# Sinks copied on chip, keys and queries as pairs of tokens, and a moved start in a fused attention and MLP kernel

## The chip, the cores and the metric

The kernel runs on one core of one Trainium2 chip. The metric is the device time of one execution in microseconds (us). The engines that matter: TensorE (PE in the rows) multiplies matrices, and transposes by multiplying with an identity; VectorE (DVE), ScalarE (ACT) and GpSimd (POOL) work elementwise; SyncE (SP) issues transfers (DMA). TensorE writes into PSUM banks, which the other engines empty.

## The reference, cut to what matters

```python
# q, k, v: 4 x 8 heads x 768 tokens x 64; n_sink = 4, window = 128
scores = q @ k.T / sqrt(64)
keep = (key < n_sink) | (0 <= query - key < window)
a = exp(where(keep, scores, -1e9) - rowmax)
a = a / (sum(a) + 1e-9)
x = (a @ v), heads side by side            # 3072 x 512
h = x @ w_in                               # 512 x 2048, float64 weights
g = h * erf(softplus(h))
out = g @ w_out                            # 2048 x 512, float64 weights
```

## The kernel before, in words

**Tiles and steps.** The 3072 tokens are 12 groups of 256. Attention works on a group's eight heads two at a time, so a group is 4 steps, 48 in all; group 0 is steps 0 to 3, group 1 steps 4 to 7. The numbers behind names (`tp_4`, `ps_4`) are steps. For the MLP a group's hidden layer is 16 chunks of 128 units, two to a PSUM bank: `h_0` holds chunks 0 and 1, `h_2` the next two, up to `h_14`; the gate of `h_0` is `gf_1`, of `h_2` `gf_3`, and so on.

**One step of attention.**
- `prep` transposes the keys and queries of 256 tokens on TensorE (`tqk`, L292) and copies them to `kq` on ScalarE (L295).
- `score` multiplies them (`ps`, L343), masks a triangle on VectorE (COPY_PREDICATED, L356), reduces each row's minimum (L361, results `neg`), and takes exponentials on ScalarE (L365, into `pst`, with row sums in `sum`). From step 3 on the scores of all steps share one PSUM bank pair, so `ps` of a step waits for the reductions of the step before.
- `norm` adds 1e-9 to the sums (L372) and inverts them (L373) on VectorE, multiplies `pst` by them (L378 on ScalarE for steps 2 to 7, VectorE otherwise), and multiplies the sinks' columns (`snk`, L384, VectorE).
- `ptrans` transposes `pst` (`tp`, L396) and `snk` (`ts`, L397) on TensorE. ScalarE copies them to `pa` (L403) and `pz` (L407, L409), and GpSimd selects triangles in both (L414). `tp` and `ts` share two PSUM banks of their kind with `tqk`.
- `av` multiplies by the values (`v_early`, and `vz`, which holds sinks and window halves; L451); `xfin` copies the result to `xf` on ScalarE (L464).

**The MLP.** `hidden` (L639 for group 0, which works in plain fp32; L643 for the others) makes `h` in two PSUM banks; `act` makes the gate with five ScalarE squares and the like (L656 to L661) and three products per bank on VectorE (L665), of which the first reads `h`, so that its end frees the bank for the `h` after next. `project` (L685 for groups 0 and 1) adds into the output banks.

**Weights.** They lie in 8-byte words. 32 blocks of 512 KB are loaded on SP's queue (`ws`), and VectorE makes fp32 of each 128x512 block by three instructions: one TENSOR_SCALAR (L541, "first conversion" below) and two SCALAR_TENSOR_TENSOR (L546, L549). Each block has two halves, so a block is listed as `wf_N` from `ws_N`. This conversion runs through the first 100 us, between the attention's instructions on VectorE.

**The start.** For groups 0 and 1, `early_load` brings keys, queries and values with 256-byte pieces; `early_sinks` brings the 4 sinks' rows (16 lanes each) into `vz` by eight small DMAs, and `early_dup` copies halves of `vz` on GpSimd.

**What sets the order.** `plan` gives each stage of each step a due slot, `at` turns the slot and the stage's offset (`O`, and `E` for slots below `EA`) into a priority, and a list of stages sorts inside one slot. A scheduler then orders each engine's instructions at build time by these priorities and its own estimate of times; `follow` pins one instruction behind another on its engine. Engines run their queues in order.

## Time and profile before

| | us |
|---|---|
| median of 3 runs | 741.97 (741.89 to 742.29) |
| the profiled execution | 741.58 |
| its span | 739.5 |
| TensorE busy | 716.2 (97% of the span) |
| ScalarE busy | 552.0 (75%) |
| VectorE busy | 486.6 (66%) |
| GpSimd busy | 204.8 (28%) |
| granted TensorE clock, mean | 0.994 |

The busy shares are means over a start of some 100 us, in which VectorE is full and TensorE waits now and then, and a long rest, in which TensorE is always busy. The rows below are of the start. In a timeline row the number in brackets at the end is the time for which that engine idled before the row, and the name behind the arrow is what released it. A row with "x16" holds sixteen instructions in a row, and its duration runs from the first one's start to the last one's end; one multiplication in fp32 shows as two instructions, a transpose as one. As instructions overlap in the pipeline, the time of one is best read from start to start.

### The profile page before, as it was taken

To read this page: it belongs to the slowest core of one execution; us is meant where nothing else is said; L and a number is where in the kernel's file an instruction comes from. 1 tells how busy PE (TensorE), PEld (TensorE's weight loads), DVE (VectorE), ACT (ScalarE), POOL (GpSimd) and SP (SyncE) were. 2 spreads that over 40 slices of the span, in tenths; PEclk is the share of its full clock that TensorE was granted. 3 is DMA by queue.
4 is the path that set the end of the run, shared out by engine and by line. 5 is a ranking of instruction groups with operands and counts; after the bars stand their busy time and mean duration, and the time that the engine had idled before them with its cause. 6 is when DMAs were issued, how large, how long until landed. Compare 5 with 4: busy or idle time off the path is not lost. (4 is left out here: it accounts for less than half of the span.)

```text
span 739.5 us, 16417 instructions
## 1 busy us (share of the span) xinstructions
PE 716.2 (97%) x5808; PEld 596.2 (81%) x5808; DVE 486.6 (66%) x1367; ACT 552.0 (75%) x1313; POOL 204.8 (28%) x302
## 2 busy tenths in 40 slices
PE   6779899999999999999999999999999999999997
PEld 3556567766888888888888888888888888899885
DVE  8899987765786675665666665665666566475252
ACT  5676759974986966976885975976886886776573
POOL 3311132111332432332233242234224223333221
PEclk9899999999999999999999999999999999999999
DMA  7998011122212222212212311211221221200000
GB/s 182 319 373 305 16 35 47 32 54 47 73 40 58 66 47 54 64 37 55 75 34 55 82 38 44 76 41 39 77 52 37 79 55 38 63 17 2 29 1 34
DMA packets 113001, 53.07 MB, mean 72 GB/s; under 512 B 91728, under 2 KB 105552, under 8 KB 112912
## 3 DMA queue, kind: packets, MB, share of 16 engines
q1 hardware_dynamic: 112352, 51.87, 26.0%
q8 instruction: 49, 0.80, 0.5%
q14 instruction: 40, 0.33, 0.2%
q10 hardware_dynamic: 560, 0.07, 0.1%
HBM read 38.01 MB, written 6.29 MB: 60 GB/s over the span
## 5 line engine op out<-in xcount | busy, mean ns | idle before, releaser
L643 PE MATMUL h<-xh,wt 128*128 128x256 f32 x1408 | 277.8, 285 | 0.2 <-DVE u L665 0.2
L643 PEld LDWEIGHTS h<-xh,wt 128*128 128x128 f32 x1408 | 223.9, 188 | 7.0 <-issue 1.1
L673 POOL TENSOR_TENSOR g<-u,g 128x512 fp32r<-128x512 f32 x80 | 106.0, 1325 | 340.6 <-DVE g L672 336.9
L643 PE MATMUL h<-xl,wt 128*128 128x256 f32 x704 | 197.8, 282 | 0.0
L661 ACT ACTIVATE u<-r 128x512 f32<-128x512 f32 x288 | 161.6, 622 | 10.3 <-DVE gf L665 3.1
L643 PEld LDWEIGHTS h<-xl,wt 128*128 128x128 f32 x704 | 132.1, 188 | 4.8 <-issue 1.0
L665 DVE SCALAR_TENSOR_TENSOR u<-u,u 128x512 f32<-128x512 f32 x160 | 125.6, 785 | 14.9 <-ACT u L661 0.9
L689 PE MATMUL o<-wt,g 128*128 128x512 f32 x320 | 127.4, 398 | 0.0
L688 PE MATMUL o<-wt,g 128*128 128x512 f32 x320 | 127.3, 398 | 0.0
L690 PE MATMUL o<-wt,g 128*128 128x512 f32 x320 | 123.6, 397 | 0.2 <-POOLq L811 0.2
L665 DVE SCALAR_TENSOR_TENSOR u<-u,h 128x512 f32<-128x512 f32 x80 | 54.9, 686 | 83.1 <-ACT u L661 80.6
L414 POOL TENSOR_SCALAR_AFFINE_SELECT pz<-pa 64x256 f32<-64x256 f32 (+1 forms) x96 | 50.9, 530 | 157.1 <-ACT pa L403 153.8
L365 ACT ACTIVATE pst<-pst,neg 128x144 f32<-128x144 f32 x192 | 77.5, 407 | 19.3 <-DVE neg L361 18.3
L656 ACT ACTIVATE r<-h 128x512 f32<-128x512 f32 x96 | 56.7, 590 | 20.3 <-PE h L643 15.7
L688 PEld LDWEIGHTS o<-wt,g 128*128 128x128 f32 x320 | 60.0, 187 | 11.5 <-ACT ot L694 0.4
L690 PEld LDWEIGHTS o<-wt,g 128*128 128x128 f32 x320 | 59.0, 187 | 12.5 <-POOLq L811 0.7
L689 PEld LDWEIGHTS o<-wt,g 128*128 128x128 f32 x320 | 60.0, 188 | 10.6
L672 DVE CAST g<-u 128x512 fp32r<-128x512 f32 x80 | 34.8, 434 | 47.5 <-PE o L690 44.7
L657 ACT ACTIVATE r<-r 128x512 f32<-128x512 f32 x96 | 60.7, 632 | 2.6
L658 ACT ACTIVATE r<-r 128x512 f32<-128x512 f32 x96 | 60.7, 632 | 2.5
L685 PE MATMUL o<-wf,gf 128*128 128x512 f32 x128 | 58.8, 595 | 1.7 <-DVE gf L665 1.7
L295 ACT COPY kq<-tqk 128x512 f32<-128x512 f32 x48 | 27.9, 582 | 36.3 <-PE tqk L292 34.1
(88 smaller groups left out, 938.0 us busy)
## 6 DMA issues: line engine op xcount, KB each, us to landing
ws<-in_moe_w_in_dram SPq DMA_DIRECT2D x16, 512.0 KB, 7.2
ws<-in_moe_w_out_dram SPq DMA_DIRECT2D x16, 512.0 KB, 8.2
out_dram<-ot SPq DMA_DIRECT2D x24, 256.0 KB, 2.3
v<-in_v_dram SPq DMA_DIRECT2D x56, 96.0 KB, 2.2
q<-in_q_dram SPq DMA_DIRECT2D x80, 64.0 KB, 2.1
k<-in_k_dram SPq DMA_DIRECT2D x80, 64.0 KB, 2.1
vz<-v SPq DMA_DIRECT2D x80, 64.0 KB, 2.1
kq<-kq SPq DMA_DIRECT2D x28, 64.0 KB, 2.0
```

Of the source, the lines that this page charges most:

```text
L365: nc.scalar.activation(y, y, AF.Exp, bias=d["neg"][:, i, h : h + 1], scale=-1.0, accum_out=d["sum"][:, i, h : h + 1])
L643: last = nc.tensor.matmul(o, wt[NC * j + c][:, p, fs], xt[e][:, c, :], start=(m == 0), stop=(m == len(ops) - 1))
L656: nc.scalar.activation(r, h, AF.Tanh, bias=b_t, scale=0.5)
L657: nc.scalar.activation(r, r, AF.Square, bias=b_v, scale=-0.5)
L658: nc.scalar.activation(r, r, AF.Square, bias=b_r)
L661: sq = nc.scalar.activation(u, r, AF.Square, bias=b_a[i], scale=CS)
L665: pr = nc.vector.scalar_tensor_tensor(out=acc, in0=u, scalar=CC[i] * CS**2, in1=x, op0=ALU.add, op1=ALU.mult)
L673: nc.gpsimd.tensor_tensor(gl, acc, gh.bitcast(F32), op=ALU.subtract)
L685: nc.tensor.matmul(o, gt[0][:, ws], wf[16 + f], start=(f == 0), stop=(f == NF - 1))
L688: behind(nc.tensor.matmul(o, gh[:, ws], wt[16 + f][:, 0, :], start=(f == 0), stop=False))
L689: nc.tensor.matmul(o, gh[:, ws], wt[16 + f][:, 1, :], start=False, stop=False)
L690: nc.tensor.matmul(o, gl[:, ws], wt[16 + f][:, 0, :], start=False, stop=(f == NF - 1))
```

## The change

1. **Sinks.** Four of the eight sink DMAs are gone; GpSimd copies the rows from the other half of `vz` (`early_dup`, z = 2). The zero fill of that half is dropped.
2. **Pairs of tokens.** Group 1's keys and queries are loaded with two neighbouring tokens on a partition, in two DMAs of 512-byte pieces instead of four of 256-byte pieces. `prep` turns them with eight ordinary matmuls per step, 64 output partitions each, in alternate halves, instead of four transposes, and ScalarE puts them in order with two strided copies instead of one.
3. **Step 1 first on ScalarE.** Step 2's `norm` moves behind `ptrans` in its slot (`norm2`); `follow` puts step 2's multiplies behind step 1's `pz` copies, step 3's exponentials behind step 2's multiplies, and step 2's transposes behind step 0's values.
4. **Slots.** `ptrans` of steps 4 to 7 is due one slot later, `prep` of steps 4 and 5 is due in slot 5 instead of 4, and `EA` goes from 12 to 6.
5. **The addition of 1e-9** for steps 4 to 7 goes from VectorE to ScalarE.

```diff
-PW, EA = 256, 12
+PW, EA = 256, 6
...
-            nc.vector.memset(vz[: P // 2, 1], 0.0)
...
+                if nm != "v" and g:
+                    t = t.rearrange("p (h j d) -> p h j d", h=H, j=2)
...
+                if nm != "v" and g:
+                    x = src[0, hs, g * GT : (g + 1) * GT].rearrange("h (p j) d -> p h (j d)", j=2)
+                    nc.sync.dma_start(t[:, hs].rearrange("p h j d -> p h (j d)"), x)
+                    return
...
-                if z:
+                if z == 2:
+                    nc.gpsimd.tensor_copy(vz[lo, 1], vz[hi, 0])
+                elif z:
...
+                if g == 1:
+                    prev = None
+                    for n, t in enumerate((d["k"], d["q"])):
+                        for j in range(2):
+                            for h in range(2):
+                                prev = follow(prev, nc.tensor.matmul(
+                                    tp[64 * h : 64 * h + 64, 2 * n + j, :], t[:, h, j], ident, start=True, stop=True
+                                ))
+                    for n in range(2):
+                        y = kq[:, c, 1 + 2 * n : 3 + 2 * n, :P].rearrange("p b (t j) -> p b j t", j=2)
+                        nc.scalar.copy(y, tp[:, 2 * n : 2 * n + 2, :].rearrange("p j (b t) -> p b j t", b=2))
+                    return
...
-                        nc.scalar.activation(
+                        follow(mark["n"] if s == 3 else None, nc.scalar.activation(
...
-                follow(mark["t", 2] if s == 1 else None, nc.vector.tensor_scalar_add(sm, sm, 1.0e-9))
+                if NE <= s < NA:
+                    nc.scalar.activation(sm, sm, AF.Identity, bias=1.0e-9)
+                else:
+                    follow(mark["t", 2] if s == 1 else None, nc.vector.tensor_scalar_add(sm, sm, 1.0e-9))
...
-                            nc.scalar.mul(p, p, sm[:, i, h : h + 1])
+                            mark["n"] = follow(mark["z"] if s == 2 else None, nc.scalar.mul(p, p, sm[:, i, h : h + 1]))
...
-                        mark["p", s] = nc.tensor.transpose(out=tp[:, h, i, :], in_=pst[:, s % RING, i, h, :P], identity=ident)
+                        x = nc.tensor.transpose(out=tp[:, h, i, :], in_=pst[:, s % RING, i, h, :P], identity=ident)
+                        mark["p", s] = follow(mark["v"] if s == 2 else None, x)
...
-                    nc.scalar.copy(pz[hf, :, :, other], y.broadcast_to([HP, 2, 2, HP]))
+                    mark["z"] = nc.scalar.copy(pz[hf, :, :, other], y.broadcast_to([HP, 2, 2, HP]))
...
-                prev = mark.get(("p", s + 1)) if 0 < s < NE - 1 else None
+                prev = mark.get(("p", s + 1)) if s == 2 else None
...
+                mark["v"] = prev
...
-                        ("prep", prep, max(4, s - 1) if NE <= s < 2 * NPAIR else pos(s) - 3), ("norm", norm, pos(s) + 1 + (s == 1)), ("ptrans", ptrans, pos(s) + 2),
+                        ("prep", prep, max(5, s - 1) if NE <= s < 2 * NPAIR else pos(s) - 3), ("norm" if s != 2 else "norm2", norm, pos(s) + 1 + (s == 1)), ("ptrans", ptrans, pos(s) + 2 + (NE <= s < 2 * NPAIR)),
...
-            STAGES = ("xfin", "norm", "ptrans", "av", "kcopy", "prep", "core", "dup", "load")
+            STAGES = ("xfin", "norm", "ptrans", "norm2", "av", "kcopy", "prep", "core", "dup", "load")
...
-            head += [(early_sinks, z, i, h) for z in range(2) for i in range(2) for h in range(2)]
+            head += [(early_sinks, 0, i, h) for i in range(2) for h in range(2)]
...
-            for z in range(2):
+            for z in range(3):
                 plan.setdefault(0, []).append(("kcopy", lambda s: early_dup(s), z))
```

The order shows what the moves come to. First ScalarE's queue behind the exponentials of step 2, before:

```order
L365 ACTIVATE pst_132,sum_2_304<-pst_132,neg_2_305 128x144 x4
L464 COPY xf_0_408<-av_0_362 128x256
L378 ACTIVATE pst_132<-pst_132,sum_2_304 128x128 x4
L403 COPY pa_1_351<-tp_1_344 128x512
L409 COPY pz_1_352<-tp_1_344 64x2x64
L365 ACTIVATE pst_132,sum_3_376<-pst_132,neg_3_377 128x144
L407 COPY pz_1_352<-ts_1_345 64x4x64 x2
L365 ACTIVATE pst_132,sum_3_376<-pst_132,neg_3_377 128x144 x3
L403 COPY pa_2_425<-tp_2_418 128x512
```

and after the change (line numbers of the changed kernel are higher; L403, L378, L365 and L464 are L430, L404, L388 and L492 there):

```order
L388 ACTIVATE pst_131,sum_2_298<-pst_131,neg_2_299 128x144 x4
L430 COPY pa_1_337<-tp_1_330 128x512
L436 COPY pz_1_338<-tp_1_330 64x2x64
L434 COPY pz_1_338<-ts_1_331 64x4x64 x2
L404 ACTIVATE pst_131<-pst_131,sum_2_298 128x128 x4
L388 ACTIVATE pst_131,sum_3_370<-pst_131,neg_3_371 128x144 x4
L404 ACTIVATE pst_131<-pst_131,sum_3_370 128x128 x4
L492 COPY xf_0_402<-av_0_356 128x256
L430 COPY pa_2_419<-tp_2_412 128x512
```

Step 1's three copies stand ahead of step 2's four multiplies, the four exponentials of step 3 behind these, and the copy of step 0's output (`xf_0`) behind step 3's multiplies.

Next VectorE's queue around the masked copies of step 4's scores (`ps_4`) and the first of the four reductions, before:

```order
L541 TENSOR_SCALAR wf_16_579<-ws_16_183 128x512
L546 SCALAR_TENSOR_TENSOR wf_6_558<-ws_7_178,wf_6_558 128x512
L546 SCALAR_TENSOR_TENSOR wf_16_579<-ws_16_183,wf_16_579 128x512
L356 COPY_PREDICATED ps_4_539<-tri_125,ps_4_539 64x2x2x64
L549 SCALAR_TENSOR_TENSOR wf_6_558<-ws_7_178,wf_6_558 128x512
L541 TENSOR_SCALAR wf_16_579<-ws_17_272 128x512
L549 SCALAR_TENSOR_TENSOR wf_16_579<-ws_16_183,wf_16_579 128x512
L356 COPY_PREDICATED ps_4_539<-tri_125,ps_4_539 64x2x2x64
L541 TENSOR_SCALAR wf_18_609<-ws_18_274 128x512
L546 SCALAR_TENSOR_TENSOR wf_16_579<-ws_17_272,wf_16_579 128x512
L361 ISA pst_132,neg_4_538<-ps_4_539,mask_78 128x144
```

and after:

```order
L569 TENSOR_SCALAR wf_8_655<-ws_8_400 128x512
L574 SCALAR_TENSOR_TENSOR wf_18_607<-ws_19_394,wf_18_607 128x512
L574 SCALAR_TENSOR_TENSOR wf_8_655<-ws_8_400,wf_8_655 128x512
L577 SCALAR_TENSOR_TENSOR wf_18_607<-ws_19_394,wf_18_607 128x512
L379 COPY_PREDICATED ps_4_553<-tri_125,ps_4_553 64x2x2x64
L569 TENSOR_SCALAR wf_8_655<-ws_9_447 128x512
L577 SCALAR_TENSOR_TENSOR wf_8_655<-ws_8_400,wf_8_655 128x512
L569 TENSOR_SCALAR wf_10_680<-ws_10_453 128x512
L379 COPY_PREDICATED ps_4_553<-tri_125,ps_4_553 64x2x2x64
L574 SCALAR_TENSOR_TENSOR wf_8_655<-ws_9_447,wf_8_655 128x512
L574 SCALAR_TENSOR_TENSOR wf_10_680<-ws_10_453,wf_10_680 128x512
L384 ISA pst_131,neg_4_552<-ps_4_553,mask_78 128x144
```

The blocks `wf_18` (from `ws_18` and `ws_19`), `wf_8` and part of `wf_10` now stand ahead of the first reduction: between step 3's sinks and that reduction there are 12 first conversions and 22 second or third ones, where there were 8 and 13.

Last TensorE's queue around step 4's transposes (`tp_4`), where `ps_5` is the scores of step 5, before:

```order
L343 MATMUL ps_5_622<-kq_128 64x224 x2
L396 MATMUL tp_4_590<-ident_61,pst_132 128x128 x2
L639 MATMUL h_4_816<-xf_0_408,wf_4_467 128x256 x2
L639 MATMUL h_4_816<-xf_0_408,wf_6_558 128x256 x2
L639 MATMUL h_4_816<-xf_0_408,wf_4_467 128x256 x2
L639 MATMUL h_4_816<-xf_0_408,wf_6_558 128x256 x2
L396 MATMUL tp_4_590<-ident_61,pst_132 128x128 x2
L397 MATMUL ts_4_591<-ident_61,snk_4_576 128x128
L685 MATMUL o_0_0_852<-wf_16_579,gf_1_713 128x512
```

and after:

```order
L366 MATMUL ps_5_636<-kq_128 64x224 x2
L422 MATMUL tp_4_618<-ident_61,pst_131 128x128 x3
L667 MATMUL h_4_830<-xf_0_402,wf_4_449 128x256 x2
L667 MATMUL h_4_830<-xf_0_402,wf_6_572 128x256 x2
L667 MATMUL h_4_830<-xf_0_402,wf_4_449 128x256 x2
L667 MATMUL h_4_830<-xf_0_402,wf_6_572 128x256 x2
L422 MATMUL tp_4_618<-ident_61,pst_131 128x128
L424 MATMUL ts_4_619<-ident_61,snk_4_590 128x128
L366 MATMUL ps_6_762<-kq_128 64x208 x2
L366 MATMUL ps_6_762<-kq_128 64x224 x2
```

Three of the four transposes of step 4 now stand ahead of `h_4`, and the scores of step 6 ahead of the first output products (`o`).

## Rows read from the trace of the kernel before

**Rows 1.** Table of stretches: us, busy time of each engine (instructions), granted clock, DMA share, GB/s.

```profile
24.00:25.00 1.00, 0.21 (x2) 0.21 (x4) 1.00 (x2) 1.00 (x6) 0.87 (x3) 0.67 1.04 208
25.00:31.00 6.00, 6.00 (x38) 4.74 (x37) 5.64 (x13) 4.18 (x12) 2.51 (x6) 0.50 0.97 312
31.00:32.00 1.00, 1.00 (x7) 0.79 (x6) 1.00 (x3) 0.00 (x0) 0.00 (x0) 0.92 1.31 259
100.00:120.00 20.00, 20.00 (x152) 13.96 (x151) 14.97 (x46) 14.11 (x38) 5.41 (x8) 1.00 0.14 31
```

**Rows 2.** Timeline of TensorE: start, duration, engine, line, operation, tiles, [idle before].

```profile
22.73 0.66 PE L396 MATMUL tp<-ident,pst 128*128 128x128 f32 x4 [2.55 <-ACT pz L409]
24.79 0.70 PE L451 MATMUL av<-pa,v_early 128*64 128x128 f32 x4 [1.40 <-POOL pa L414]
...
34.59 0.44 PE L292 MATMUL tqk<-ident,k_early 128*128 128x128 f32 x2
34.86 0.38 PE L292 MATMUL tqk<-ident,q_early 128*128 128x128 f32 x2
...
36.29 0.64 PE L451 MATMUL av<-pz,vz 128*64 128x64 f32 x16
36.86 5.45 PE L639 MATMUL h<-xf,wf 128*128 128x256 f32 x24
...
45.83 0.62 PE L396 MATMUL tp<-ident,pst 128*128 128x128 f32 x2 [2.61 <-ACT pst L378]
46.33 3.72 PE L639 MATMUL h<-xf,wf 128*128 128x256 f32 x16
...
52.07 3.70 PE L685 MATMUL o<-wf,gf 128*128 128x512 f32 x8 [1.69 <-DVE gf L665]
...
75.87 0.33 PE L396 MATMUL tp<-ident,pst 128*128 128x128 f32 x1 [1.61 <-ACT pst L378]
```

**Rows 3.** The same of TensorE, from 78 us on.

```profile
91.97 3.29 PE L639 MATMUL h<-xf,wf 128*128 128x256 f32 x14 [0.49 <-DVE gf L665]
```

**Rows 4.** Timeline of VectorE from 25 to 46 us.

```profile
25.77 0.38 DVE L384 TENSOR_TENSOR snk<-pst,sum 128x128 f32<-128x128 f32 x1
...
30.09 0.43 DVE L541 TENSOR_SCALAR wf<-ws 128x512 int32<-128x512 int32 x1 [0.23 <-DMA ws<-in_moe_w_in_dram]
...
34.75 0.43 DVE L541 TENSOR_SCALAR wf<-ws 128x512 int32<-128x512 int32 x1 [1.49 <-DMA ws<-in_moe_w_out_dram]
...
39.93 0.31 DVE L361 CUSTOM_DVE_ANT_0 pst<-ps,mask 128x144 f32<-128x144 f32 x1
...
42.05 0.42 DVE L541 TENSOR_SCALAR wf<-ws 128x512 int32<-128x512 int32 x1
42.39 0.68 DVE L549 SCALAR_TENSOR_TENSOR wf<-ws,wf 128x512 int32<-128x512 int32 x1
42.99 0.42 DVE L541 TENSOR_SCALAR wf<-ws 128x512 int32<-128x512 int32 x1
...
45.60 0.68 DVE L665 SCALAR_TENSOR_TENSOR gf<-u,h 128x512 f32<-128x512 f32 x1
```

**Rows 5.** Timeline of ScalarE from 19 to 46 us.

```profile
19.42 0.37 ACT L464 COPY xf<-av 128x256 f32<-128x256 f32 x1
...
40.28 0.41 ACT L365 ACTIVATE pst<-pst,neg 128x144 f32<-128x144 f32 x1 [2.93 <-DVE neg L361]
...
41.88 0.58 ACT L656 ACTIVATE r<-h 128x512 f32<-128x512 f32 x1
...
45.40 0.97 ACT L378 ACTIVATE pst<-pst,sum 128x128 f32<-128x128 f32 x3
```

**Rows 6.** Timeline of GpSimd from 12 to 26 us.

```profile
16.64 0.68 POOL L414 TENSOR_SCALAR_AFFINE_SELECT pz<-pa 64x128 f32<-64x128 f32 x2 [0.79 <-ACT pa L403]
...
22.59 1.45 POOL L414 TENSOR_SCALAR_AFFINE_SELECT pz<-pa 64x128 f32<-64x128 f32 x2 [3.30 <-ACT pa L403]
```

More of the change, by code (lines that the diff above doesn't have):

```diff
@@ L42 @@
 NM, NA = 2, 8
-PW, EA = 256, 12
-O = dict(prep=-100, norm=-100, core=-300, av=-300, load=-400, dup=-100, kcopy=-50, ptrans=-200, xfin=-100,
+PW, EA = 256, 6
+O = dict(prep=-100, norm=-100, norm2=-100, core=-300, av=-300, load=-400, dup=-100, kcopy=-50, ptrans=-200, xfin=-100,
          hid=0, proj=900, res=500, act=-400, wl=100, wc=0, ws=300)
@@ L223, in early_tile @@
                 t = wpool.tile([P, 2 * DM], F32, tag="wo", name=f"{nm}_early{g}")
-                t = early[g, nm] = t.rearrange("p (n h d) -> p n h d", n=2, h=H)
+                if nm != "v" and g:
+                    t = t.rearrange("p (h j d) -> p h j d", h=H, j=2)
+                else:
+                    t = t.rearrange("p (n h d) -> p n h d", n=2, h=H)
+                early[g, nm] = t
                 for c in range(NPAIR):
@@ L228, in early_tile @@
                         d[nm] = [early[0, nm][:, 1, cs] if g else None] + [t[:, n, cs] for n in range(2)]
+                    elif g:
+                        d[nm] = t[:, cs]
                     else:
@@ L364, in score @@
                         )
-                        nc.scalar.activation(
+                        follow(mark["n"] if s == 3 else None, nc.scalar.activation(
                             y, y, AF.Exp, bias=d["neg"][:, i, h : h + 1], scale=-1.0, accum_out=d["sum"][:, i, h : h + 1]
-                        )
+                        ))
             def norm(s):
@@ L371, in norm @@
                 sm = d["sum"]
-                follow(mark["t", 2] if s == 1 else None, nc.vector.tensor_scalar_add(sm, sm, 1.0e-9))
+                if NE <= s < NA:
+                    nc.scalar.activation(sm, sm, AF.Identity, bias=1.0e-9)
+                else:
+                    follow(mark["t", 2] if s == 1 else None, nc.vector.tensor_scalar_add(sm, sm, 1.0e-9))
                 nc.vector.reciprocal(sm, sm)
```

## The prediction

> **What bounds the kernel now.** I read the table of stretches first. From 100 to 120 us TensorE is busy 20.00 of 20 us [rows 1], and from 92 us to the last output it hardly waits. So the time is TensorE's work plus its waits in the first 92 us plus what the half clock costs there, and the reader should look for these two things only.
>
> TensorE's timeline gives the waits. The bracket at a row is the idle time before it. At 22.73 it is 2.55 us (step 1's copies on ScalarE), at 24.79 1.40 (GpSimd's selects), at 45.83 2.61 (step 4's normalised scores), at 52.07 1.69 (the gate of group 0), at 75.87 1.61 [rows 2], and at 91.97 0.49 [rows 3]. That is 10.35 us. After the first two the granted clock is 0.67, then 0.50 from 25 to 31 us, then 0.92 [rows 1]. 0.50 is the lower of its two levels, 1.2 of 2.4 GHz. What is missing to full speed sums to 0.33 + 6 x 0.50 + 0.08 = 3.4 us.
>
> Then VectorE's timeline. It works through the queue of weight conversions almost without a pause; two waits for the DMA, 0.23 and 1.49 us [rows 4], are all it has between step 3's sinks (25.77) and the gate at 45.60. So a place in VectorE's queue is a time, and counting instructions there gives due times. ScalarE, the third view, waits for VectorE at 40.28, 2.93 us, for step 4's reductions [rows 5].
>
> **The change at the start (to 28 us).** Step 1's copies go ahead of step 2's multiplies and of step 3's exponentials on ScalarE; TensorE takes the transposes of step 1 before step 0's products. In the trace of before the 2.55 us wait was for these copies, so it goes. What is late next: step 0's products wait for GpSimd, which now selects for step 1 behind step 0's pair, a wait I put at 1.4 us (a pair of selects takes 0.68, or 1.45 beside conversions [rows 6]). And the copy of step 0's output, at 19.42 in before (0.37 us [rows 5]), now stands behind the multiplies of step 3 on ScalarE, near 27.0; the first hidden product waits for it, 2.9 us. So 3.95 us of waits become about 4.3: no gain, at least none here. The clock may stay up, which would gain up to 3.4 at this place; whether it matters is decided later, since TensorE runs into VectorE's next result anyway.
>
> **Fewer DMAs.** Four sink copies and two loads go from SP's queue. The weights arrive some 2 us earlier (an estimate), and VectorE's two waits, 1.72 us, vanish. GpSimd gets one more copy, while it is idle. The dropped fill costs VectorE nothing.
>
> **Pairs of tokens.** Step 4 to 7's keys and queries are turned by eight half-width products instead of four transposes. Two transposes start 0.27 us before the next two, so four take 0.54 [rows 2]. The nearest rows for the new form: eight 64-column half-width products (16 records) take 0.57 us (36.29 to 36.86), at 128 columns 1.14 per step; not overlapped at all, half of a full-width 256-column product, 5.45 us / 12 / 2 = 0.23 each, 1.8 per step [rows 2]. So 0.6 to 1.3 us more per step, 2.4 to 5.0 in all; I take 2.4, since the products with alternate halves in the rows do overlap. It lies in 28 to 41 us, in front of TensorE's wait for step 4, which has room for it: in before TensorE idled 2.61 us there, and the change lengthens that wait (next part). If that cover is gone, it costs its 2.4. ScalarE copies twice at about 0.37 (the 128x256 copy) instead of once; it idles there.
>
> The Trainium skill bears on this: "TensorEngine Tiling (Array Packing)", Restrictions and Gotchas, says that column tiling can't be used with the transpose mode for fp32 input. So pairs in halves must run as ordinary fp32 products, as the order shows; the rows above price this, and the rule gives no other time.
>
> **Step 4's place in VectorE's queue: the term that decides.** The transposes of steps 4 to 7 come one slot later, step 4's preparation too, and the scheduler fills VectorE with weights before step 4's reductions. From step 3's sinks to the first reduction stand in before 8 first conversions, 13 second or third ones and 2 masked copies; after the change 12, 22 and 2. A first conversion takes 0.34 us (42.05 to 42.39), another 0.60 (42.39 to 42.99), a masked copy some 0.40 (an estimate between these two), a reduction 0.23 [rows 4]. Before: 11.3 us by this count, 26.08 + 11.3 + 1.72 of DMA waits = 39.1, against 39.93 measured, so the count runs 0.85 short. After: 18.0, so 44.1 by bare count, 45.0 with the 0.85, 45.5 with it in proportion. I take 45.0: five us later than 39.93.
>
> From there two chains lead to the first hidden product of chunk 4, at 46.33 in before [rows 2].
> - Scores: from the first exponential (40.28) to the first multiply (45.40) ScalarE took 5.12 us; one square (0.58) leaves that stretch, the sum's addition comes onto ScalarE (some 0.2; between nothing and the 0.37 of a small copy) [rows 5]: 4.7. So 45.3 + 4.7 = 50.0, then 0.43 to the first transpose [rows 2]; the new order wants three transposes instead of two, whose third multiply ends 0.65 later (0.97 for three): 51.1.
> - Gate: the bank that it writes is free when VectorE's first product of the gate is done, in before 45.60 + 0.6. The count for it after is 15, 27, 3 masked copies, 4 reductions and small ones, 23.4 us: 26.08 + 23.4 + 0.6 = 50.1 bare, 51.1 with the shortfall.
>
> Both say about 51.1 for what stood at 46.33: **+4.8 us**. Bounds: 50.1 by bare counts, +3.7; 51.6 in proportion, +5.2.
>
> **After that.** Of before's waits 1.69 + 1.61 + 0.49 = 3.8 lay behind 46.33. The new order puts step 6's scores ahead of the first output products. They have one score bank, so they wait for step 5's reductions: count 28.3, plus four reductions, 55.3 bare, 56.5 with a shortfall of 1.2; TensorE is free at 55.1 (four us of work behind 51.1): 1.4 us idle. Then output products from 57.5. Twelve of them (0.9), sixteen hidden ones (0.45) and some 4 us of small ones [rows 2] bring it to 79.4 us; the hidden product it then needs waits for the gate of chunk 7, 78.3 bare, 80.4 with a shortfall: 1.0 idle. The next gate (83.2 bare, about 86 with the shortfall) costs another 0.9. Sum: +4.8 - 3.8 + 1.4 + 1.0 + 0.9 = **+4.3**. TensorE's idle 41.5 to 50 us, with one short set of scores between, may also drop the clock; a stretch at half clock like before's costs 3.4 at most, and the waits just named absorb most of it: I add 0.3, near the lower end. On the profiled run, 741.58, this makes 746.2; the median of the runs is 0.4 higher, so **746.6 us**. Its own range is 743.5 to 749.0, from bare counts (+2.2) to full ones with half a clock loss.
>
> **The rivals.**
> - Second stretch at the half clock, not absorbed, or transposes at 1.8 us that use up the cover: +3.4 - 0.3 on the forecast, 748 to 751. For it: 3.95 us of waits within 5 us brought the clock down in before; against: 2.61 at 45.83 did not. The Trainium skill, "TensorE: Matmul & The Clock Gate", Why this matters for your kernels, warns of a drop after an idle gap; the trace agrees at 24 us and shows none at 46.
> - Faster, by one mechanism: step 4's reductions are not late. If VectorE's first reduction of step 4 ends before about 41 us (the weights arrive earlier, and the conversions run off before the scores are needed), then 2.61, 1.69 and 1.61 shrink to little, and the clock at the start stays up (3.4 gained), against 2.4 for the pairs, 4.3 instead of 3.95 at the start and new waits of 3.3: 5.9 + 3.4 - 2.4 - 0.3 - 3.3 = 3.3 gained, 738.5. For it: VectorE's waits for the DMA vanish. Against: six more us of conversions stand in its queue.
> - No net change: the late gates wait less than counted, the new waits of 3.3 us turn out near zero: +4.8 - 3.8 = +1.0, 742.9, range 740.5 to 743.4.
> - The change doesn't do what it says: the order shows the moves, so only that the earlier sinks aren't waited for; it is in the others.
>
> **How the numbers follow.** The forecast 0.58, the half clock 0.10, no net change 0.15, faster 0.17. About 0.2%, 1.5 us, is what a measurement of this kernel can tell from none. Slower: 0.58 + 0.10 = 0.68, and 0.01 from the upper edge of no change. Range: to leave out no more than 2 in 10 it goes from 741.0 (most of the faster case outside, all of no change nearly inside) to 750.0.
>
> **What would show it.** In the profile after: the first reduction of step 4 near 45.0 (right) or under 41 (wrong, then faster); VectorE without DMA waits from 26 to 45; TensorE idle in front of step 4's transposes until 50.4, and of the first score set of step 6 near 56; eight products for the keys and queries of a step at 1.1 us; the first hidden product near 27.4; the waits at 20 and 24 us 1.4 and 2.9. Wrong would be a last idle of TensorE before 51 us, or a granted clock of 0.5 past 50 us.

## The result and the profile after

The changed kernel takes 749.79 us (748.90 to 750.55, 4 runs) against 742.03 for the kernel before: a ratio of 1.0104, 95% interval 1.0086 to 1.0121, so slower by 7.8 us. The forecast was 746.6 us, slower, in a range of 741.0 to 750.0. The profiled execution took 750.52 us with a span of 748.6, 9.1 us longer than that of before; it is one of the two longer runs of the four, and both of these lie above the upper edge of 750.0.

TensorE's timeline of the changed kernel shows where its waits now are (start, duration, engine, line, operation, tiles, idle time before the row with its releaser):

```profile
19.70 0.82 PE L422 MATMUL tp<-ident,pst 128*128 128x128 f32 x4 [1.97 <-ACT pst L388]
...
22.44 1.11 PE L478 MATMUL av<-pa,v_early 128*64 128x128 f32 x8 [1.55 <-POOL pa L441]
...
28.01 0.70 PE L667 MATMUL h<-xf,wf 128*128 128x256 f32 x2 [0.65 <-ACT xf L492]
...
30.41 0.93 PE L478 MATMUL av<-pa,v_early 128*64 128x128 f32 x8 [0.79 <-POOL pa L441]
...
34.63 0.66 PE L306 MATMUL tqk<-ident,k_early 128*64 128x128 f32 x8
35.12 0.61 PE L306 MATMUL tqk<-ident,q_early 128*64 128x128 f32 x8
...
46.90 0.99 PE L366 MATMUL ps<-kq 64*64 64x208 f32 x16 [1.21 <-DVE neg L384]
50.90 1.06 PE L422 MATMUL tp<-ident,pst 128*128 128x128 f32 x3 [3.01 <-ACT pst L404]
52.06 4.99 PE L667 MATMUL h<-xf,wf 128*128 128x256 f32 x16
...
57.57 0.99 PE L366 MATMUL ps<-kq 64*64 64x208 f32 x16 [0.30 <-DVE neg L384]
...
82.08 3.72 PE L667 MATMUL h<-xf,wf 128*128 128x256 f32 x16 [1.24 <-DVE gf L693]
...
87.13 0.34 PE L478 MATMUL av<-pa,v_early 128*64 128x64 f32 x4 [1.21 <-POOL pa L441]
87.95 0.55 PE L478 MATMUL av<-pa,v_early 128*64 128x128 f32 x8 [0.48 <-POOL pa L441]
```

Against [rows 2] and [rows 3]: the wait of 2.55 us for step 1's copies is gone, the selects' wait is 1.55 instead of 1.40. The first products of `h_4`, at 46.33 in before, start at 52.06, behind a wait of 3.01 for step 4's multiplies, and take 4.99 instead of 3.72 us. Behind that stand 0.30, 1.24, 1.21 and 0.48, where before had 1.69, 1.61 and 0.49. The clock tells why `h_4` is slow (table of stretches; the granted clock is the third number from the end):

```profile
22.00:24.00 2.00, 1.56 (x22) 1.22 (x24) 2.00 (x10) 2.00 (x9) 1.74 (x5) 0.50 1.14 348
24.00:28.00 4.00, 3.36 (x37) 2.73 (x35) 3.86 (x10) 2.55 (x11) 0.36 (x2) 0.58 1.09 359
28.00:32.00 4.00, 3.20 (x31) 2.19 (x31) 4.00 (x8) 2.88 (x9) 3.16 (x7) 0.85 0.88 245
32.00:36.00 4.00, 4.00 (x36) 3.20 (x36) 4.00 (x9) 0.60 (x2) 1.21 (x3) 0.72 0.96 367
47.00:51.00 4.00, 0.99 (x17) 0.59 (x17) 3.97 (x10) 4.00 (x13) 0.00 (x0) 1.00 1.05 280
51.00:55.00 4.00, 3.90 (x11) 2.80 (x12) 3.94 (x9) 3.74 (x9) 0.00 (x0) 0.57 1.03 316
88.00:92.00 4.00, 4.00 (x17) 3.28 (x18) 4.00 (x8) 3.26 (x6) 0.00 (x0) 0.60 0.00 0
```

In [rows 1] one stretch at the lower level, 1.2 GHz, lay between 24 and 32 us. Now there are three: 22 to 36 us with an interruption, 51 to 55 after the 3.01 us wait, and 88 to 92 after the two waits for GpSimd's selects. What is missing to full speed, summed as busy time times (1 - clock) over one-us stretches, is 4.2, 1.7 and 1.7 us, against 3.2 in before.

VectorE's timeline has step 3's sinks, the first reduction of step 4, the first gate product, the last reduction of step 5 and the gate product that frees the bank for `h_10`:

```profile
26.29 0.29 DVE L410 TENSOR_TENSOR snk<-pst,sum 128x128 f32<-128x128 f32 x1
...
28.97 0.53 DVE L569 TENSOR_SCALAR wf<-ws 128x512 int32<-128x512 int32 x1
...
45.76 0.31 DVE L384 CUSTOM_DVE_ANT_0 pst<-ps,mask 128x144 f32<-128x144 f32 x1
...
51.24 0.67 DVE L693 SCALAR_TENSOR_TENSOR gf<-u,h 128x512 f32<-128x512 f32 x1
...
57.11 0.30 DVE L384 CUSTOM_DVE_ANT_0 pst<-ps,mask 128x144 f32<-128x144 f32 x1
...
81.35 0.68 DVE L693 SCALAR_TENSOR_TENSOR gf<-u,h 128x512 f32<-128x512 f32 x1
```

Between 26 and 46 us no row has a wait for the DMA; in [rows 4] there were 0.23 and 1.49 us. The profile lists no wait of VectorE at all from 26 to 90 us. The first reduction comes at 45.76 instead of 39.93, the gate product at 51.24 instead of 45.60. On ScalarE the first exponential follows at 46.11 and the first multiply of step 4 at 50.46, where [rows 5] had 40.28 and 45.40.

**The ledger.** From before to after, `h_4` starts 5.73 us later. From there on its half clock costs 1.31 (4.84 us of work at a granted clock of 0.73; the other 0.36 of that stretch fell on the transposes in front of it and is part of the 5.73). The waits behind it are 0.30 + 1.24 + 1.21 + 0.48 = 3.23, and the third half clock costs 1.70. Before's waits of 3.79 behind 46.33 are gone. The sum is 8.2 of the 9.1 us; I have no row for the rest.

The ledger says where the time stands, not what each entry would give back. VectorE waits for nothing from 26 to 90 us, so two starts on TensorE are set by VectorE's queue: step 6's scores at 57.57, behind step 5's last reduction at 57.11, and `h_10` at 82.08, behind the gate product at 81.35. `h_4` at full clock would, by these rows, only have made TensorE wait longer in front of 57.57. Seen over the whole span, TensorE idles 23.3 us in before and 25.1 after (span less busy time, 748.6 less 723.5). Of its 7.3 us more of busy time 4.4 are the lower clock.

### The profile page after: what moved, and what is told of

It is laid out like the page before. It is cut to its first block, busy times and chain, and to the rows that moved or that the text cites. A ratio compares the mean times of both kernels' runs of the same rounds, so it can differ in the third digit from the quotient of the medians.

```text
span 748.6 us, 16504 instructions
## 1 busy us (share of the span) xinstructions
PE 723.5 (97%) x5856; PEld 601.0 (80%) x5856; DVE 486.3 (65%) x1362; ACT 553.8 (74%) x1321; POOL 206.0 (28%) x303
## 5 line engine op out<-in xcount | busy, mean ns | idle before, releaser
L388 ACT ACTIVATE pst<-pst,neg 128x144 f32<-128x144 f32 x192 | 77.5, 408 | 22.2 <-DVE neg L384 21.2
L441 POOL TENSOR_SCALAR_AFFINE_SELECT pz<-pa 64x256 f32<-64x256 f32 (+1 forms) x96 | 47.8, 498 | 166.1 <-ACT pa L430 162.8
L430 ACT COPY pa<-tp 128x512 f32<-128x512 f32 x48 | 28.2, 587 | 36.7 <-PE tp L422 36.7
```

The source lines that it names most:

```text
L388: follow(mark["n"] if s == 3 else None, nc.scalar.activation(y, y, AF.Exp, bias=d["neg"][:, i, h : h + 1], scale=-1.0, accum_out=d["sum"][ ...
```

## The experiments

Two theories stood at first. **Q:** step 4's place behind conversions in VectorE's queue sets the time. **P:** the pairs' own work on TensorE does, or the new start. A third one, **L**, came out of the first four runs. Times of before beside the runs were 741.8 to 742.2 us. In the diffs `...` leaves out lines.

**e1: step 4 pulled forward in the changed kernel.** No weight block from the 11th on may begin before step 4's last reduction.

```diff
                 follow(mark.get(("c", wn - 2)), first)
+                if wn >= 11:
+                    follow(mark["t", 4], first)
```

> The changed kernel with one order rule more: the first instruction of weight block 11 and of all later ones stands behind step 4's last reduction on VectorE. Between step 3's sinks and step 4's first reduction VectorE then has 8 first and 16 other conversions instead of 12 and 22. Everything else of the change stays. Theory Q (step 4's place in VectorE's queue sets the time): first reduction of step 4 at about 40.9 us instead of 45.76 (scores end at 39.1 and bound it), first products of h_4 near 47.3 instead of 52.06, the half-clock stretch at 51 to 55 us gone: 743 to 745.5 us. Theory P (the pairs' eight products and the start's new waits are what costs, TensorE work and not the queue): no change beyond 1 us from 749.8.

Measured: 751.88 us median, four runs of 752.06, 751.71, 746.21 and 752.14. Neither theory has a place for three runs 5.5 to 5.9 us above the fourth. The profiled run is one of the long ones. GpSimd's timeline in it, and VectorE's beside it:

```profile
28.48 10.92 POOL L441 TENSOR_SCALAR_AFFINE_SELECT pz<-pa 64x128 f32<-64x128 f32 x2 [3.83 <-ACT pa L430]
39.47 0.68 POOL L441 TENSOR_SCALAR_AFFINE_SELECT pa<-pa 64x128 f32<-64x128 f32 x2
```

```profile
28.94 0.42 DVE L569 TENSOR_SCALAR wf<-ws 128x512 int32<-128x512 int32 x1
...
36.37 1.30 DVE L576 SCALAR_TENSOR_TENSOR wf<-ws,wf 128x512 int32<-128x512 int32 x2
37.57 1.30 DVE L579 SCALAR_TENSOR_TENSOR wf<-ws,wf 128x512 int32<-128x512 int32 x2
```

Two selects that take 0.68 us at 39.47 took 10.92 from 28.48 on. VectorE converted without a pause until 38.87, and the selects ended 0.5 us after that. Behind them on GpSimd stood the others of steps 2 and 3, and TensorE waited 9.56 us for them at 39.82. So this says nothing firm on Q: the run of 746.21 us, 0.7 above Q's range, has no profile.

**e2: the changed kernel with a filler.** Idle transposes in the queue between step 5's scores and step 4's transposes.

```diff
+                if s == 4:
+                    x = nc.tensor.matmul(tp[:, 0, 0, :4], ident, d["neg"].rearrange("p i h -> p (i h)"), start=True, stop=True)
+                    for _ in range(22):
+                        x = follow(x, nc.tensor.transpose(out=tp[:, 0, 0, :], in_=ident, identity=ident))
```

> The changed kernel with 22 idle transposes of the identity (some 3 us) put into TensorE's queue between step 5's scores and step 4's transposes, where it idles 3.01 us; a later write overwrites their result. VectorE's queue is the same up to step 6's reductions. If the low clock from 51 to 55 us comes from that idle time and costs 1.7 us: granted clock 1.00 from 47 to 58 us, h_4 still starts near 52, takes 3.7 instead of 4.99 us, time about 748.0 us. If the clock's drop costs nothing at the end (absorbed by the waits behind it, as the prediction put it): 749.8 within 0.5 us. If the drop comes from elsewhere: clock still 0.5 there.

Measured: 754.12 us (753.40 to 754.83). The same pair of selects took 13.39 us here, and TensorE waited 12.03 for it; the filler then ran at full clock from 58.32 to 60.76 and `h_4` took 3.63 us, but at 61.15. The question on the clock's price stayed open and was put again in e9.

**e3: pairs undone.** Loads and transposes of group 1 as before (the four conditions on group 1 set to false).

> The changed kernel with group 1's keys and queries loaded and transposed as before. VectorE has 11 first and 19 other conversions ahead of step 4's reductions (12 and 22 with pairs). Theory Q: the first reduction some 2 us earlier, near 43.7 us, h_4 near 50, 746 to 748 us. Theory P (pairs): 742 to 744 us, since TensorE gets back its work and the scores of step 4 come earlier.

Measured: 745.73 us (744.01 to 747.74), ratio 1.0061 (1.0039 to 1.0083). Undoing the pairs gives back 4.1 of the 7.8 us. By the times alone neither expectation is met: the five runs spread over 3.7 us, the median lies 0.3 us below Q's range and 1.7 above P's, and the profiled run is at P's edge. The rows of the profiled run are Q's: the first reduction of step 4 comes at 43.68 (43.7 expected) and `h_4` at 49.56 (50), behind the gate product.

```profile
49.56 6.75 PE L667 MATMUL h<-xf,wf 128*128 128x256 f32 x16 [3.40 <-DVE gf L693]
```

The pair products themselves are cheap: rows 34.63 and 35.12 of after start 0.49 us apart at a lowered clock, and in e6 at full clock two sets of eight start 0.44 apart, so a step takes 0.88 against 0.54 us for four transposes, 1.4 us more for four steps.

**e4: slots undone.**

```diff
-PW, EA = 256, 6
+PW, EA = 256, 12
...
-                        ("prep", prep, max(5, s - 1) if NE <= s < 2 * NPAIR else pos(s) - 3), ("norm" if s != 2 else "norm2", norm, pos(s) + 1 + (s == 1)), ("ptrans", ptrans, pos(s) + 2 + (NE <= s < 2 * NPAIR)),
+                        ("prep", prep, max(4, s - 1) if NE <= s < 2 * NPAIR else pos(s) - 3), ("norm" if s != 2 else "norm2", norm, pos(s) + 1 + (s == 1)), ("ptrans", ptrans, pos(s) + 2),
```

> The changed kernel with the slots of before (transposes of steps 4 to 7 one slot earlier, preparation of steps 4 and 5 in slot 4, EA 12); the rest of the change stays. VectorE still has 12 first and 20 other conversions ahead of step 4's reductions, the output products stand ahead of step 6's scores again. Theory Q: first reduction near 44.6 us, h_4 near 51: 747.5 to 749.5 us. Rival (the later slots are what made step 4 late, as the prediction's wording has it): 741 to 744 us.

Measured: 750.93 us, four runs of 751.29, 750.97, 746.54 and 750.88. The profile of 751.29 shows the long select again, 11.59 us at 28.53. All four runs lie outside both expectations. What the slots are worth isn't settled by this.

**e5: two pauses for GpSimd (theory L).** L: VectorE's unbroken conversions keep a select from finishing. Two copies of two columns read the last select of steps 2 and 3, and later blocks stand behind them.

```diff
+                if s in (2, 3):
+                    z = small.tile([P, 2], F32, tag="gap", name=f"gap_{s}")
+                    mark["gap", s] = nc.vector.tensor_copy(z[hi], pa[hi, 1, 1, P - 2 :])
...
                 follow(mark.get(("c", wn - 2)), first)
+                if wn >= 5:
+                    follow(mark["gap", 2], first)
+                if wn >= 7:
+                    follow(mark["gap", 3], first)
```

> The changed kernel with two tiny VectorE copies that read the last select of step 2 and of step 3, placed behind three and six more weight blocks after step 3's sinks, so that VectorE pauses until GpSimd is through. New theory L: in three kernels (changed with held blocks, with filler, without slots) one pair of GpSimd selects took 11 to 13 us while VectorE ran conversions without a pause, and TensorE waited for it 7.8 to 12.0 us. If L is right: both select groups end within 2.5 us of their start, TensorE's wait there is under 2 us, and runs lie within 1 us of each other; VectorE loses at most 2 us, first reduction of step 4 at 45 to 47 us (theory Q keeps it there, 12 first and 21 other conversions ahead), time 748 to 750.5 us. If pauses don't matter to GpSimd: waits of 7 us or more again in some runs, spread of 4 us and more.

Measured: 746.79 us (746.13 to 747.26). GpSimd's and TensorE's timelines:

```profile
28.43 1.41 POOL L441 TENSOR_SCALAR_AFFINE_SELECT pz<-pa 64x128 f32<-64x128 f32 x2 [3.84 <-ACT pa L430]
29.91 0.68 POOL L441 TENSOR_SCALAR_AFFINE_SELECT pa<-pa 64x128 f32<-64x128 f32 x2
```

```profile
30.27 0.71 PE L481 MATMUL av<-pa,v_early 128*64 128x128 f32 x8 [0.72 <-POOL pa L441]
...
47.55 1.16 PE L366 MATMUL ps<-kq 64*64 64x208 f32 x16 [3.62 <-DVE neg L384]
52.30 6.74 PE L674 MATMUL h<-xf,wf 128*128 128x256 f32 x16 [3.60 <-DVE gf L700]
```

The first pair takes 1.41 us and the second 0.68, VectorE paused 0.94 us, and TensorE's wait is 0.72. The runs lie within 1.1 us. That is as L has it, but the changed kernel's own profile has no long select either; the test of L is e6 beside e1, and e9 beside e2. The time missed the expected 748 to 750.5 us: it is 3.0 us under the changed kernel although the first reduction comes even later (46.40). `h_4` starts at 52.30, 0.24 later than there, and takes 1.75 us longer, but the waits of 3.23 and the third half clock of 1.70 behind it are gone, since the rest of the order came out another way: 2.9 us in all. The gate product that frees the bank for `h_10` stands behind 43 second or third conversions (counted from step 3's sinks) here, where it was 49.

**e6: pauses and step 4 pulled forward.** The edits of e1 and e5 together.

> The two pauses of the kernel before together with the rule that holds weight block 11 and later ones behind step 4's last reduction (8 first and 16 other conversions ahead of it, 12 and 21 with pauses alone). Theory Q, now without the disturbance of L: first reduction of step 4 at 40.5 to 42.5 us, h_4 near 47.5, no half clock behind 45 us, 743.5 to 746 us, 4 us or more under the kernel with pauses alone. Theory P (pairs' TensorE work and the start): the same time as with pauses alone, within 1 us.

Measured: 743.92 us (743.66 to 744.27, 10 runs), ratio to before 1.0020 (1.0010 to 1.0029). It is 2.9 us under e5, from which it differs by the hold alone. From e1 it differs by the pauses alone: none of the ten runs has the 5.5 us and more that three of four had there, which bears L out.

```profile
42.02 0.31 DVE L384 CUSTOM_DVE_ANT_0 pst<-ps,mask 128x144 f32<-128x144 f32 x1
```

```profile
33.88 0.61 PE L306 MATMUL tqk<-ident,q_early 128*64 128x128 f32 x8
34.32 0.61 PE L306 MATMUL tqk<-ident,k_early 128*64 128x128 f32 x8
...
46.42 0.91 PE L422 MATMUL tp<-ident,pst 128*128 128x128 f32 x3 [1.04 <-ACT pst L404]
...
50.77 6.07 PE L676 MATMUL h<-xf,wf 128*128 128x256 f32 x16 [2.57 <-DVE gf L702]
```

The first reduction comes 4.4 us earlier than in e5, the transposes of step 4 wait 1.04 us and go at 46.42. `h_4` gains only 1.5 us and starts at 50.77 where 47.5 was expected, since it now waits 2.57 us for the other chain, the gate product. That shows both chains of the prediction at work. The half clock was expected to be gone, but from 50 to 56 us 2.4 us are still missing. The gain of 2.9 us for step 4's place speaks for Q, though it is less than the 4 expected; P would have had no change.

**e7: start undone.** Step 2's `norm` in its old stage (that line is not shown here), and the order rules with it.

```diff
-                        follow(mark["n"] if s == 3 else None, nc.scalar.activation(
+                        follow(None, nc.scalar.activation(
...
-                            mark["n"] = follow(mark["z"] if s == 2 else None, nc.scalar.mul(p, p, sm[:, i, h : h + 1]))
+                            mark["n"] = follow(None, nc.scalar.mul(p, p, sm[:, i, h : h + 1]))
...
-                        mark["p", s] = follow(mark["v"] if s == 2 else None, x)
+                        mark["p", s] = follow(None, x)
...
-                prev = mark.get(("p", s + 1)) if s == 2 else None
+                prev = mark.get(("p", s + 1)) if 0 < s < NE - 1 else None
```

> The changed kernel with the start's order of before (norm of step 2 in its old stage, no extra order rules, step 3's exponentials and step 0's output copy where they were). VectorE has 13 first and 23 other conversions ahead of step 4's reductions. Theory Q: first reduction at 45 to 47 us and 748 to 751 us, as changed. Rival S (the new start is what costs: step 2's selects come at 28.5 us instead of 25.7): 743 to 745 us. By L, step 3's selects can still be held off, since no DMA wait of VectorE is left.

Measured: 744.80 us (743.92 to 745.08), ratio 1.0029 (1.0019 to 1.0039). By its time this is the rival's range, and Q's expectation missed. The first reduction is at 46.88, later than in the changed kernel, as Q had it; but `h_4`, in front of step 4's transposes in this order, starts at 50.70, and no wait stands behind it. So the place of the first reduction alone doesn't give the time.

```profile
50.70 6.13 PE L667 MATMUL h<-xf,wf 128*128 128x256 f32 x16 [1.59 <-DVE gf L693]
```

The end of `h_4` does, where nothing waits behind it. In e3, e5 and e7 TensorE waits for nothing from `h_4` to 140 us. `h_4` ends at 56.31, 59.04 and 56.83 there, late by its half clock too, and from that end to the end of the span it is 686.0, 686.4 and 686.4 us. In the changed kernel it is 691.6 (57.05 to 748.6): 5.2 us more, where 3.23 of waits and 1.70 of half clock stand behind `h_4`.

**e8: sinks undone.** Eight sink DMAs, the fill, no copy.

> The changed kernel with all eight sink DMAs and the fill back. The weights come later, so VectorE should wait for the DMA again between 27 and 36 us (0.23 and 1.49 us in before), which by L lets GpSimd through; 12 first and 20 other conversions stand ahead of step 4's reductions. Theory Q: first reduction at 45 to 47 us, 748 to 750 us, and no wait of TensorE for a select over 2 us. Rival (the dropped DMAs are the cause, by moving the weights forward): 742 to 744.5 us.

Measured: 743.85 us (742.91 to 745.72), ratio 1.0023 (1.0013 to 1.0032). VectorE again waits for the DMA (0.57, 0.67 and 0.27 us from 33 to 38 us), and the selects get through in 1.08. The first reduction is at 45.53, but the gate product stands behind 12 first and 22 other conversions instead of 15 and 27, and `h_4` starts at 48.39:

```profile
45.53 0.31 DVE L383 CUSTOM_DVE_ANT_0 pst<-ps,mask 128x144 f32<-128x144 f32 x1
...
47.65 0.68 DVE L692 SCALAR_TENSOR_TENSOR gf<-u,h 128x512 f32<-128x512 f32 x1
```

```profile
46.67 1.77 PE L365 MATMUL ps<-kq 64*64 64x208 f32 x16 [5.05 <-DVE neg L383]
48.39 4.78 PE L666 MATMUL h<-xf,wf 128*128 128x256 f32 x16
...
53.77 3.70 PE L712 MATMUL o<-wf,gf 128*128 128x512 f32 x8 [0.38 <-DVE gf L692]
```

Here, too, Q's expectation of the time missed, by 4 us, and the time lies in the rival's range. I had set it by the first reduction. In this order step 4's transposes stand behind `h_4`, so that `h_4` needs only the scores of step 5 and the first gate product, which both end near 48.4. That the dropped DMAs are the cause, as the rival has it, is not shown by this: putting them back also changed the order of TensorE and VectorE.

**e9: the clock by itself.** The pauses of e5 and 24 transposes of e2's filler.

> The changed kernel with the two pauses and with 24 idle transposes (3.2 us) behind step 5's scores, where TensorE idled 3.60 us in front of h_4 at 52.30. VectorE's queue is the same up to step 6's reductions. Measures the clock by itself, now without the long select. If the low clock is worth what the trace of the kernel with pauses shows (3.36 us missing from 36 to 62 us, h_4 taking 6.74 instead of 3.72 us, no wait behind it): granted clock 1.00 there and 743.3 to 744.5 us, against 746.8. If the waits behind absorb it, as the prediction put it: 746 to 747 us.

Measured: 746.05 us (745.83 to 746.14), 0.74 under e5. TensorE's timeline:

```profile
47.86 1.77 PE L366 MATMUL ps<-kq 64*64 64x208 f32 x16 [3.60 <-DVE neg L384]
...
50.00 4.71 PE L423 MATMUL tp<-ident 128*128 128x128 f32 x24
54.55 3.62 PE L678 MATMUL h<-xf,wf 128*128 128x256 f32 x16
```

The clock fell already during the 3.60 us wait in front of step 5's scores, so that the filler ran at half clock and took 4.71 us instead of some 3. `h_4` starts 2.25 us later than in e5 and takes 3.62 instead of 6.74 us, so it ends 0.87 us earlier, and the kernel is 0.74 faster by the medians (1.4 between the two profiled runs). The expected 743.3 to 744.5 missed, since the filler came after the drop. The time lies in the range that I had given to the other answer, 746 to 747 for a clock that is absorbed. With only 0.87 us to give back, and runs of e5 that spread over 1.1, this run can't decide between the two. The ends of `h_4` in e3, e5 and e7 say more: what `h_4` loses there goes through, since TensorE waits for nothing behind it.

**e10: pairs alone.** The kernel before with the pairs' loads, products and copies.

> The kernel before with only the pairs of tokens (loads, half-width products, two copies). VectorE has 10 first and 17 other conversions ahead of step 4's reductions (8 and 13 before), and 13 and 23 ahead of the first gate product (11 and 19). Theory Q: first reduction near 42.5 us, h_4 near 49, clock perhaps down once: 744 to 747 us. If only the products' own time counted (0.35 us per step more in the changed kernel's trace, 1.4 in all) and were covered: 741.5 to 743.5 us.

Measured: 745.91 us (745.28 to 746.03), ratio 1.0052 (1.0035 to 1.0069).

```profile
42.40 0.31 DVE L383 CUSTOM_DVE_ANT_0 pst<-ps,mask 128x144 f32<-128x144 f32 x1
```

```profile
48.33 0.77 PE L421 MATMUL tp<-ident,pst 128*128 128x128 f32 x2 [3.19 <-ACT pst L403]
48.89 5.02 PE L666 MATMUL h<-xf,wf 128*128 128x256 f32 x16
```

The reduction (42.5 expected, 42.40), `h_4` (49 and 48.89) and the drop of the clock came as Q has it. Pairs alone cost 3.8 us. The products' own 1.4 lie in front of a wait of 3.19 us, which covers them. `h_4` starts 2.6 us later than in before and takes 1.3 longer, behind two more first conversions and four more others ahead of step 4; the waits behind it are 1.2 us less, and the last us has no row.

**e11: step 4 pulled forward in the kernel before.** The edit of e1 with 9 in place of 11, made to the kernel before.

> The kernel before with one order rule: weight block 9 and later ones behind step 4's last reduction on VectorE (6 first and 12 other conversions ahead of it instead of 8 and 13; 10 and 18 ahead of the first gate product instead of 11 and 19). Theory Q used the other way: first reduction near 38.6 us instead of 39.93, TensorE's waits at 45.83 and 52.07 us shorter by about 1 us each: 740 to 741.5 us. If conversions ahead of step 4 don't set the time: 742 within 0.5 us.

Measured: 746.15 us (745.41 to 746.66), ratio 1.0054 (1.0037 to 1.0071), 4 us slower where it should have been faster.

```profile
45.35 0.33 PE L396 MATMUL tp<-ident,pst 128*128 128x128 f32 x1 [2.63 <-ACT pst L378]
...
46.38 5.41 PE L641 MATMUL h<-xf,wf 128*128 128x256 f32 x16
...
75.17 0.33 PE L396 MATMUL tp<-ident,pst 128*128 128x128 f32 x1 [1.68 <-ACT pst L378]
...
87.91 3.72 PE L641 MATMUL h<-xf,wf 128*128 128x256 f32 x16 [0.99 <-DVE gf L667]
...
101.02 0.38 PE L645 MATMUL h<-xh,wt 128*128 128x256 f32 x1 [1.27 <-DVE gf L667]
...
127.71 0.38 PE L645 MATMUL h<-xh,wt 128*128 128x256 f32 x1 [0.99 <-DVE gf L667]
```

The first reduction comes only 0.5 us earlier (39.43), since VectorE now waits 0.55, 0.26 and 1.24 us for the DMA; the gate product is at 45.65 as before, and `h_4` at 46.38 with it. The blocks held back are then missing later: TensorE waits 0.99, 1.27 and 0.99 us for gates, and the clock drops once more (5.41 us for `h_4`). So Q holds in one direction only. My reading is that the conversions have to be done some time, and that before's order of them was the better one; no run tests that by itself.

**e12: the new start alone, with the hold of e11, on the kernel before.**

> The kernel before with the change's new start alone (norm of step 2 behind step 1's copies and the order rules with it; no pairs, no sinks copied, old slots) and the rule of the kernel before this one. Theory Q: the start's waits of 2.55 and 1.40 us become about 1.6 and 0.6, step 4's reductions come as early as with the rule alone: 739.5 to 741.5 us. Theory L: VectorE's DMA waits are as in before, so GpSimd's selects get through; if not, a wait of 5 us and more in some runs and 745 us.

Measured: 744.63 us (744.20 to 746.66), ratio 1.0039 (1.0027 to 1.0050). It is 1.5 us under e11, so the new start may be worth something in this company; against the kernel before it is slower, and the expected 739.5 to 741.5 missed. `h_4` is at 46.34 and takes 3.72 us, as in before; of the waits behind it those for gates alone are 1.68, 1.48 and 1.65 us. Selects go through in 1.08 and 1.25 us, beside DMA waits of VectorE of 1.52, 0.30 and 1.37. None of the twelve beats the kernel before. The copied sinks, the later slots and the moved addition (part 5) were not tested by themselves.

## Why the prediction was right, and where not

- **Step 4's place in VectorE's queue** was the right term, and the count held: first reduction 45.0 predicted, 45.76 measured; `h_4` 51.1 and 52.06, both chains within 1 us (multiplies at 50.46 for 50.0, gate product at 51.24 for 50.5). e3, e10 and e6 against e5 show the mechanism up to `h_4`. The words that put it down to the later slots are not borne out: with all slots undone (e4) 12 first and 20 other conversions still stand ahead, and pairs alone (e10) bring 10 and 17 where before has 8 and 13. Which part brings how many in the whole change stays open.
- **The clock.** I put the second drop, at `h_4`, at 0.3 us, since the waits behind it would absorb it, and the rows bear that out: `h_4`'s 1.31 and the 0.30 in front of step 6's scores make 1.61, where I had 1.4 of wait and 0.3 of clock. What the sum lacks is a third drop: 1.70 us at 88 us, behind the waits of 1.21 and 0.48 for GpSimd's selects, with no wait behind it to absorb it. My own sign of being wrong, a granted clock of 0.5 past 50 us, is there twice. My rival with the second drop not absorbed, 748 to 751 us at a chance of 0.10, is where the time fell, but not by its mechanism. Before the drop at 51 us stand two waits, of 1.21 and 3.01 us with one us of work between, as 2.55 and 1.40 stand before the one in [rows 1].
- **The waits behind** sum to 3.23, predicted 3.3, which is luck: the scores of step 6 wait 0.30 (1.4) because `h_4` was slow, `h_10` waits 1.24 (1.0), and instead of a second gate (0.9) GpSimd's selects cost 1.69.
- **The start**: 1.4 and 2.9 us predicted; 1.55 and 0.65, and 0.79 and 1.97 for what I had not named (step 2's selects, and, as its row names it, ScalarE's last exponentials ahead of step 1's transposes). The sum is 4.96 for 4.3. It lies in front of the wait for step 4, as predicted. The clock did not stay up there.
- **Pairs**: 0.88 us a step instead of 1.14, 1.4 more in all instead of 2.4.
- **DMAs**: the two waits of VectorE went, as predicted. I took that as a gain; by L it also takes away the pauses in which GpSimd gets through.
- **The size.** 4.6 us were predicted for the profiled run. To that come 0.93 at `h_4`'s start, 0.79 for the selects in place of the second gate, 0.24 at `h_10` and 1.70 for the third drop, less 0.09 at the second: 8.2 of the 9.1 us. The two terms that were missing are GpSimd's wait at 87 us and the drop of the clock behind it.
- **The range** held by 0.2 us, with two of the four runs outside it. That is luck: its upper edge reaches into the rival with one more half clock, and has nothing of GpSimd in it.

## What to carry to other kernels

Where an engine is full, count the instructions ahead of a result in its queue and you have its time within a us; do it for every chain that meets at the next engine, not for the earliest one alone. Where two waits stand close together on TensorE, look for the lower clock, and ask what waits behind it: in front of a wait that another engine's queue sets it costs nothing (`h_4` in the changed kernel), and where nothing waits behind it, it costs in full (88 us there, `h_4` in e3, e5 and e7). In e6 the runs' mean granted clock goes from 0.988 to 0.996, some 6 us of TensorE's time, and their times differ by 0.6; where their drops lie only one profile shows. Taking small transfers or waits from a full engine may shift a whole schedule: undoing any one of three parts here (pairs, start, sinks) gained 4 to 6 us, and their sum is far more than the loss of 7.8, so such parts are not to be added up.

## What the runs showed of the hardware that I had not expected

A pair of GpSimd selects, 0.67 to 2.1 us in the other rows of steps 0 to 3, took 10.92, 13.39 and 11.59 us in three profiles (e1, e2, e4), each time until VectorE's row of conversions ended, and 0.5 us longer. In the other profiles the selects of steps 2 and 3 went through beside the same conversions; in the changed kernel the conversions were slower instead (a first conversion of 0.53 us at 28.97, 0.42 in e1). In e1 and e4 it came and went from run to run, 4 to 6 us apart, if the short runs are those without it; they have no profile. The Trainium skill, "SBUF — State Buffer", Who interferes with whom, says that VectorE and GpSimd contend for a shared port pair, which it calls an exclusive lock, and that a VectorE instruction with two inputs in SBUF, as the second and third conversions have, contends with a GpSimd instruction that reads SBUF. The traces agree that one holds up the other, and show more: in e1 the pair of selects did not end before 19 further conversions had. That the port pair is the reason is not shown by any run. Why one run falls to this side and another not, the rows don't tell. That a pause of VectorE ends it is shown by e6 beside e1: ten runs within 0.6 us, where three of four were 5.5 us and more above the fourth. In e9, e2's filler with the pauses, no long select is left either.
